# The first expert layer in six chunks of 384 tokens instead of nine of 256, with a chain of three steps

## The chip, the cores and the metric

The kernel runs on one core of one Trainium2 chip, as one program. The metric is the device time of one execution in microseconds (us): the median of the runs, and beside it the time of the one execution that was profiled. In the profile PE is TensorE (matmul), PEld its weight loads, DVE VectorE, ACT ScalarE, POOL GpSimd and SP SyncE.

## The reference

Three layers stand one behind the other. All inputs and results are float32.

```python
# attention: 4 batches, 8 heads, 576 tokens, head size 64, causal, with a decay bias
bias = -(cum[:, :, :, None] - cum[:, :, None, :])          # cum = cumsum(max(s, 0))
scores = where(causal, -1e9, scale * q @ k.T + minimum(bias, 0))
x = softmax(scores) @ v                                     # -> 2304 tokens x 512
# first expert layer: w_in 512 x 2048, w_out 2048 x 512, both in 64-bit floats in DRAM
h = x @ w_in
x = (h * cos(h)) @ w_out
# second layer: 8 experts, each w1 512 x 1024 and w2 1024 x 512, the best two for each token
noisy = x @ w_gate + log1p(exp(x @ w_noise)) * noise
top2, weights = best two of noisy, softmax over the two
out[token] += weight * (relu(x @ w1[e]) @ w2[e])            # for both experts e of a token
```

## The kernel before

Every float32 product is done as three passes on TensorE: each operand is split into a high part (a rounded copy that ScalarE writes) and a low part (the difference that VectorE or GpSimd writes), and high x high, high x low and low x high are summed in PSUM (`PASS`). So behind nearly each operand stand a copy on ScalarE and a subtraction on another engine.

**The order of the work** is the order in which Python issues it; each engine goes through its own list in that order. Three tables and loops set it.

- `front` (L179) runs attention: 16 pairs of heads with 5 units each, in a loop over t. Its copies to high parts are L287, the low parts L291, the copies of its results L440 and L443, its last product L437. In each turn it calls `moe.beside(t, N)` (L784), which hangs early work of the first expert layer beside it: loads and conversions of weight pieces, splits of x, and in the last turns the first six steps of the layer (one turn has two).
- `Moe1` (L710) is the first expert layer. Its unit of work, an item, is a chunk c of 256 tokens and a block f of 128 of the 2048 inner features. There are 144 items: the first three chunks are interleaved over the 16 blocks (48 items), since every new block needs weights that have just been converted; then come five chunks in order, and the last one runs backwards over f. `step()` (L918) issues one step: for item i the product L1 (L865, 12 matmuls of 256 columns), for item i-1 two copies out of PSUM on ScalarE (L879, L880) and `angle` on VectorE (L886: h minus a multiple of 2 pi), for item i-2 `cosine` on ScalarE (L890 Abs, L891 Sin with its table), for item i-3 `gate` (L895 on VectorE, L897 on ScalarE), for item i-4 `rest_of_gate` (L903 on VectorE), and for item i-LAG, LAG = 5, the product L2 (L905, two tiles of 128 tokens with three matmuls of 512 columns). Two PSUM banks hold L1's results.
- Weights of the first layer come as 64-bit floats; 32 pieces (w_in and w_out for each f) are converted in five steps in as many turns (`w_steps`, L749): Abs on ScalarE (L760), two operations on VectorE (L763, L764), two more (L767, L768), the high part on ScalarE (L773), the low part on VectorE (L778). `convert()` does the next step of each piece under way.
- When a chunk ends, `finish` (L946) copies it out, writes it to DRAM, transposes it tile by tile and makes the router's products, logits, best two, and places. `Router` works on groups of tiles (`GROUPS`), and GpSimd scatters the tokens of a group into the lists of the experts by indirect DMA (L695), two scatters for a tile.
- `Moe2` (L1039) is the second layer. A job is an expert and a number of tiles of 126 tokens from its list; each has 8 steps, one for each block of 128 inner features. A step has L1 (L1133), relu copies (L1136, L1137) and L2 (L1145); the weights of a later step are split on ScalarE (L1121) and on VectorE or GpSimd (L1122). So that the second layer can start before the first has ended, the first jobs work only on the tokens routed by then (`FIRST` tiles of 128): experts 0 and 1 with 3 tiles, then experts 2 to 7 with 5, then experts 0 and 1 again with the other 2. `meet` (L1260) joins the two layers: the last chunk's transposes, products and router work are hung on steps and tiles of the first job by a table (step, tile).

## Time and profile before

| | |
|---|---|
| median of 3 runs | 1158.11 us (1156.95 to 1158.71) |
| profiled execution | 1157.83 us, of which span 1156.1 us |
| TensorE busy | 1101.7 us (95%), 6988 instructions |
| VectorE busy | 722.2 us (62%) |
| ScalarE busy | 677.8 us (59%) |
| GpSimd busy | 474.2 us (41%) |
| moved by DMA | 148.98 MB, mean 129 GB/s |

The busy shares are means over the whole span, and the stages have different limits. Attention lasts to some 230 us, the first expert layer to some 680 us, the second to the end. Which engine sets the pace is read per stage: from the gaps on TensorE, and from what ended each.

### The profile page before, as it was taken

How to read it: one execution, taken by the hardware profiler on the slowest of the kernel's cores; microseconds unless marked ns; L12 is line 12 of the kernel's file. 1: busy time of each engine (PE TensorE's matmuls, PEld its weight loads, DVE VectorE, ACT ScalarE, POOL GpSimd, SP SyncE). 2: the span in 40 equal slices, each digit the busy share in tenths (PEclk: the TensorE clock that was granted, in tenths of full speed). 3: DMA queues.
4: the chain of work that ended last, by engine and by line, in shares of the span. 5: the costliest groups of instructions: out<-in, count | busy, mean ns of one | idle time of the engine just before them, and what ended most of it. 6: DMA issues, size and time to landing. Idle time of an engine off the chain costs nothing.

```text
span 1156.1 us, 20848 instructions
## 1 busy us (share of the span) xinstructions
PE 1101.7 (95%) x6988; PEld 972.3 (84%) x6988; DVE 722.2 (62%) x1811; ACT 677.8 (59%) x1744; POOL 474.2 (41%) x665
## 2 busy tenths in 40 slices
PE   5999889899999999999999999999999999999995
PEld 4887777787778999988898978999999989999884
DVE  5999999889988544465446676544444444445382
ACT  4999988877778666676667764423232323233241
POOL 4777877400002101006313158545454545445373
PEclk7999999999999999999999999999999999999998
DMA  6788977365552201102010347644444444434461
GB/s 170 204 224 243 260 222 217 131 175 146 156 150 44 92 1 56 42 14 57 1 56 20 101 123 211 196 142 134 133 135 133 134 135 134 138 113 135 130 209 39
DMA packets 167692, 148.98 MB, mean 129 GB/s; under 512 B 73912, under 2 KB 132696, under 8 KB 167576
## 3 DMA queue, kind: packets, MB, share of 16 engines
q1 hardware_dynamic: 154904, 119.17, 35.4%
q0 software_dynamic: 12672, 28.39, 7.9%
q8 instruction: 57, 0.93, 0.4%
q14 instruction: 59, 0.48, 0.2%
HBM read 120.50 MB, written 29.66 MB: 130 GB/s over the span
## 4 chain that ended last, share of the span: by engine, by line
PE 69%; DVE 11%; ACT 10%; issue 4%; DMA 3%; POOL 1%; SPq 1%; another core or an unknown queue 0%; POOLq 0%; DVEq 0%; ACTq 0%
PE bank L1133 18%; PE bank L1145 18%; PE bank L869 11%; PE bank L913 11%; PE bank L437 3%; PE bank L396 2%; DVE float32r L291 2%; DVE scratch L368 2%; PE bank L342 2%; ACT float32r L897 1%; PE bank L1093 1%; ACT float L891 1%; DVE float L767 1%; ACT float L760 1%; DVE float L768 1%
## 5 line engine op out<-in xcount | busy, mean ns | idle before, releaser
L1133 PE MATMUL bank<-float32r 128*128 128x252 f32 (+1 forms) x1536 | 240.5, 310 | 0.9 <-DVE float32r L1137 0.5
L1145 PE MATMUL bank<-float32r 128*126 128x512 f32 x960 | 235.5, 394 | 0.0
L1133 PEld LDWEIGHTS bank<-float32r 128*128 128x128 f32 x1536 | 230.3, 189 | 5.5 <-DVE float32r L1137 1.0
L1145 PEld LDWEIGHTS bank<-float32r 128*126 128x126 f32 x960 | 174.4, 187 | 36.5
L869 PE MATMUL bank<-float32r 128*128 128x256 f32 x1296 | 177.8, 286 | 5.4 <-ACT float L880 5.1
L869 PEld LDWEIGHTS bank<-float32r 128*128 128x128 f32 x1296 | 166.3, 190 | 17.8 <-ACT float L880 10.0
L913 PE MATMUL bank<-float32r 128*128 128x512 f32 x630 | 166.2, 394 | 2.4 <-DVE float32r L903 2.4
L1136 ACT ACTIVATE float32r<-bank 128x378 fp32r<-128x378 f32 (+1 forms) x128 | 55.7, 435 | 185.0 <-PE bank L1133 167.2
L824 POOL TENSOR_TENSOR float<-float 128x256 f32<-128x256 f32 x24 | 20.1, 845 | 274.9 <-DMA float<-xt 273.3
L1122 POOL TENSOR_TENSOR float32r<-late,float32r 128x512 fp32r<-128x512 f32 x60 | 77.8, 1297 | 128.4 <-ACT float32r L1121 127.9
L913 PEld LDWEIGHTS bank<-float32r 128*128 128x128 f32 x630 | 112.1, 189 | 21.8 <-DVE float32r L903 3.3
L1137 DVE SCALAR_TENSOR_TENSOR float32r<-bank,float32r 128x378 fp32r<-128x378 f32 (+1 forms) x128 | 61.8, 483 | 102.3 <-ACT float32r L1136 80.3
L886 DVE SCALAR_TENSOR_TENSOR float<-float 128x256 f32<-128x256 int32 x144 | 63.8, 443 | 54.7 <-ACT float L880 53.4
L287 ACT ACTIVATE float32r<-bank 128x512 fp32r<-128x512 f32 (+3 forms) x192 | 83.5, 478 | 15.7 <-PE bank L300 9.7
L1122 DVE TENSOR_TENSOR float32r<-late,float32r 128x512 fp32r<-128x512 f32 x60 | 77.7, 1294 | 24.1 <-ACT float32r L1121 24.0
L1102 DVE TENSOR_TENSOR float32r<-bank,float32r 128x504 fp32r<-128x504 f32 x40 | 27.3, 682 | 99.3 <-ACT float32r L1101 98.3
L1101 ACT ACTIVATE float32r<-bank 128x504 fp32r<-128x504 f32 x40 | 23.7, 593 | 109.8 <-PE bank L1093 103.8
L903 DVE TENSOR_TENSOR float32r<-float,float32r 128x256 fp32r<-128x256 f32 x144 | 62.5, 434 | 39.2 <-ACT float32r L897 35.5
L379 ACT ACTIVATE scratch<-scratch 128x256 f32<-128x256 f32 (+2 forms) x144 | 82.9, 583 | 6.2 <-POOL scratch L282 6.2
L388 POOL TENSOR_SCALAR scratch<-scratch 128x256 f32<-128x256 f32 (+2 forms) x144 | 82.7, 587 | 5.8 <-DVE scratch L386 2.1
L291 DVE TENSOR_TENSOR float32r<-bank,float32r 128x512 fp32r<-128x512 f32 (+4 forms) x160 | 81.8, 539 | 4.4 <-ACT float32r L287 3.2
L897 ACT ACTIVATE float32r<-float 128x256 fp32r<-128x256 f32 x144 | 58.5, 406 | 43.6 <-DVE float L895 41.6
(155 smaller groups left out, 1929.7 us busy)
## 6 DMA issues: line engine op xcount, KB each, us to landing
late<-in_moe_w_dram SPq DMA_DIRECT2D x120, 256.0 KB
float<-negcum SPq DMA_DIRECT2D x15, 768.0 KB
float<-in_moe_w_dram SPq DMA_DIRECT2D x40, 256.0 KB
xt<-scratch SPq DMA_DIRECT2D x32, 288.0 KB
float<-in_moe_w_in_dram SPq DMA_DIRECT2D x16, 512.0 KB
float<-in_moe_w_out_dram SPq DMA_DIRECT2D x16, 512.0 KB
float<-xt SPq DMA_DIRECT2D x48, 128.0 KB
float<-negcum SPq DMA_DIRECT2D x32, 144.0 KB
```

The lines of the kernel that those rows point to most:

```text
L287: nc.scalar.activation(hi, src, AF.Copy, scale=1.0 if sc is None else sc)
L291: nc.vector.tensor_tensor(lo, src, hi.bitcast(F32), ALU.subtract)
L379: nc.scalar.activation(sc, sc, AF.Exp, bias=m, scale=-1.0, accum_out=sm[:, hh, 0:1])
L388: nc.gpsimd.tensor_scalar(sc, sc, r[:, hh:hh + 1], 1.0, op0=ALU.mult, op1=ALU.mult)
L869: self.nc.tensor.matmul(ps, w[a][:, 128 * k:128 * k + 128], self.xs[c, k][b], start=(n == 0), stop=(n == 11))
L886: nc.vector.scalar_tensor_tensor(r, n, -TWO_PI, h, op0=ALU.mult, op1=ALU.add)
L897: nc.scalar.activation(h, r, AF.Copy)
L903: self.nc.vector.tensor_tensor(l, r, h.bitcast(F32), ALU.subtract)
L913: self.nc.tensor.matmul(self.acc[c][t], g[a][:, 128 * t:128 * t + 128], w[b], start=(first and n == 0), stop=(last and n == 2))
L1122: (nc.vector if kind else nc.gpsimd).tensor_tensor(l, r, h.bitcast(F32), ALU.subtract)
L1133: nc.tensor.matmul(ps, w[a][:, 128 * k:128 * k + 128], self.xT[q][b][:, k, c], start=(m == 0), stop=(m == 11))
L1145: self.nc.tensor.matmul(self.acc[q][t], h[a][:, ROWS * t:ROWS * t + ROWS], w[b], start=(f == 0 and n == 0), stop=(f == FB - 1 and n == 2))
```

## The change

The first layer's chunk gets 384 tokens (`CH`, three tiles, `TN`), so that there are six chunks and 96 items: two interleaved chunks (32 items), three in order, and the last one backwards. L1 has 12 matmuls of 384 columns, L2 nine of 512. The chain from L1 to L2 has three steps instead of five: `gate` and `high` of item i-2, `angle` and `cosine` of item i-1, `rest_of_gate` of item i-2 and L2 of item i-3 stand in one step, in a new order. The four conversion operations on VectorE go together, and one piece is begun per step. Attention's last five turns take one step each. The splits of x follow the new chunk size, and attention's buffers lie elsewhere to make room.

The router takes groups of 9, 3, 3 and 3 tiles. `finish` transposes by blocks of 128 features (three tiles in one bank); the router's products sum up over these blocks in one bank of their own, which logits, counts and totals use too (`list_bank`). The second layer's early jobs are experts 0 to 2 with two tiles each, and three later jobs take the rest of these experts with three tiles each: 11 jobs of 8 steps instead of 10. The last chunk's router work has three tiles, six scatters, in one place of the table.

```diff
-EARLY = 3 * ROWS
+EARLY = 2 * ROWS
 LIST = 2432
 SPARE = (LIST - CAP) // 128
-WORDS_R, WORDS, SHARED = 32800, 10400, 9200
-FIRST = 14
+WORDS_R, WORDS, SHARED = 33040, 9416, 10300
+CH, TN = 384, 3
+FIRST = 12
+SPLIT = 3
...
-    def products(self, bank, x):
-
-        ps = bank[:, 0:256]
...
+    def products(self, bank, k, x):
+
+        for a in range(2):
+            self.nc.tensor.matmul(bank[:, 0:CH], self.wg[:, k], x[a], start=(k + a == 0), stop=(k + a == 4))
+        if k == 3:
+            self.nc.scalar.activation(self.terms, bank[0:32, 0:CH], AF.Copy)
...
-                for e in range(2):
+                for e in range(SPLIT):
...
-    LAG = 5
+    LAG = 3
     PRE = 2
     ORDER = tuple(range(9))
-    GROUPS = {4: 10, 6: 4, 7: 2, 8: 2}
+    NC = 6
+    GROUPS = {2: 9, 3: 3, 4: 3, 5: 3}
...
-        self.items = [(c, f) for f in range(16) for c in range(3)] + [(c, f) for c in range(3, 8) for f in range(16)]
-        self.items += [(8, f) for f in range(15, -1, -1)]
-        self.at0 = {c: min(i for i, x in enumerate(self.items) if x[0] == c) for c in range(9)}
-        self.end = {c: max(i for i, x in enumerate(self.items) if x[0] == c) for c in range(9)}
+        last = self.NC - 1
+        self.items = [(c, f) for f in range(16) for c in range(2)]
+        self.items += [(c, f) for c in range(2, last) for f in range(16)] + [(last, f) for f in range(15, -1, -1)]
...
         def b():
             nc.vector.tensor_scalar(cf, cf, EXP_LO, EXP_HI, op0=ALU.max, op1=ALU.min)
             nc.vector.tensor_scalar(c, c, 3, 0x3FFFFFF8, op0=ALU.logical_shift_left, op1=ALU.bitwise_and)
-
-        def d():
             nc.vector.scalar_tensor_tensor(c, hi, TOP2, c, op0=ALU.bitwise_and, op1=ALU.bitwise_or)
             nc.vector.scalar_tensor_tensor(c, lo, 29, c, op0=ALU.logical_shift_right, op1=ALU.bitwise_or)
+            if last:
+                self.arena.free(self.rawtile[j])
...
-        return [a, b, d, e, g]
+        return [a, b, e, g]
...
-        for _ in range((1, 1, 1, 2, 1)[t - N + 2] if t >= N - 2 else 0):
+        if t >= N - 2:
             self.step()
...
+        run(self.gate, 2)
         run(self.copy, 1)
         run(self.L1, 0)
-        while len(self.conv) < 4 and self.nconv in self.raw and self.nconv < min(32, self.PRE + (2 * i + 2) // 3 + 2):
+        while len(self.conv) < 4 and self.nconv in self.raw and self.nconv < min(32, self.PRE + i + 3):
             self.conv.append(self.w_steps())
-        run(self.rest_of_gate, 4)
+        run(self.high, 2)
+        run(self.angle, 1)
+        run(self.cosine, 1)
+        run(self.rest_of_gate, 2)
         self.convert()
-        run(self.cosine, 2)
-        run(self.gate, 3)
-        run(self.angle, 1)
         run(self.L2, self.LAG)
...
+    def list_bank(self):
+        if not hasattr(self, "ps_p"):
+            self.ps_p = Banks(self.arena, 1)
+        return self.ps_p.tile()
...
+                steps = [ops[j:j + per] for j in range(0, len(ops), per)] + [place + adv]
+                steps += [scat[j:j + 2] for j in range(0, len(scat), 2)]
...
-    JOBS = [(e, 0, 3) for e in range(2)] + [(e, 0, 5) for e in range(2, E_)] + [(e, EARLY, 2) for e in range(2)]
+    JOBS = [(e, 0, 2) for e in range(SPLIT)] + [(e, 0, 5) for e in range(SPLIT, E_)]
+    JOBS += [(e, EARLY, 3) for e in range(SPLIT)]
...
+        if moe.i == N + 1:
+            moe.ps_h.close()
             E.step(0)
...
-    for at, fns in {(1, 0): (lambda: tr(0), lambda: tr(1), lambda: sp(0), lambda: sp(1), *moe.rest[0]), (1, 2): [lambda: E.blank(E.oldp)] * 6,
-                    (2, -1): (pr, moe.fin.close), (2, 1): (lg,), (2, 2): (head,), (3, -1): moe.rest[1], (3, 3): (ops("top"),),
-                    (4, 2): (ops("place"), ops("scat")), (5, 3): (ops("adv"), close)}.items():
+    for at, fns in {(1, 0): (each(tr, 0, 1), each(sp, 0, 1)), (1, 2): [lambda: E.blank(E.oldp)] * 6,
+                    (2, -1): (each(pr, 0, 1), each(tr, 2, 3), each(sp, 2, 3)), (3, -1): (each(pr, 2, 3), moe.fin.close),
+                    (3, 1): (lg,), (3, 2): (head,), (4, 2): (ops("top"),),
+                    (5, 2): (ops("place"), ops("adv"), ops("scat")), (5, 3): (close,)}.items():
```

**ScalarE at the end of attention.** In the rows before, L287 and L440 are attention's copies, L879 and L880 copies of item 0, L760 and L773 the weights' Abs and high parts.

```order
L287 ACTIVATE float32r<-bank_73 128x3x128
L879 ACTIVATE float_88<-bank_76 128x256
L880 ACTIVATE float_88<-bank_76 128x256
L760 ACTIVATE float_88<-float_88 128x512
L287 ACTIVATE float32r<-bank_74 128x8x64
L287 ACTIVATE float32r<-bank_75 128x2x64
L440 ACTIVATE scratch<-bank_80 128x2x256
L773 ACTIVATE float32r<-float_88 128x512 x2
```

After, the same attention copies are L289 and L442, those of item 0 L896 and L897; L907 and L908 are item 0's cosine, L767 and L780 the weights.

```order
L289 ACTIVATE float32r<-bank_73 128x3x128
L896 ACTIVATE float_88<-bank_76 128x384
L897 ACTIVATE float_88<-bank_76 128x384
L907 ACTIVATE float_88<-float_88 128x384
L908 ACT_TABLE_LOAD
L908 ACTIVATE float_88<-float_88 128x384
L780 ACTIVATE float32r<-float_88 128x512 x2
L767 ACTIVATE float_88<-float_88 128x512 x2
L289 ACTIVATE float32r<-bank_74 128x8x64
L289 ACTIVATE float32r<-bank_75 128x2x64
L442 ACTIVATE scratch<-bank_80 128x2x256
```

The cosine of item 0, with its table, and two high parts and two Abs of weights moved ahead of the three last copies shown.

**VectorE in the interleaved stretch.** Before, conversions (L763, L764, L767, L768, L778) and the gate's operations (L895, L886, L903) alternate, with two of a conversion's four operations in one step.

```order
L763 TENSOR_SCALAR float_88<-float_88 128x512
L764 TENSOR_SCALAR float_88<-float_88 128x512
L895 TENSOR_TENSOR float_88<-float_88 128x256
L886 SCALAR_TENSOR_TENSOR float_88<-float_88 128x256
L903 TENSOR_TENSOR float32r<-float_88,float32r 128x256
L767 SCALAR_TENSOR_TENSOR float_88<-float_88 128x512
L768 SCALAR_TENSOR_TENSOR float_88<-float_88 128x512
```

After, a step has gate (L912), angle (L903), rest of gate (L923), a low part (L785) and all four operations of the next piece.

```order
L912 TENSOR_TENSOR float_88<-float_88 128x384
L903 SCALAR_TENSOR_TENSOR float_88<-float_88 128x384
L923 TENSOR_TENSOR float32r<-float_88,float32r 128x384
L785 TENSOR_TENSOR float32r<-float_88,float32r 128x512
L770 TENSOR_SCALAR float_88<-float_88 128x512
L771 TENSOR_SCALAR float_88<-float_88 128x512
L772 SCALAR_TENSOR_TENSOR float_88<-float_88 128x512
L773 SCALAR_TENSOR_TENSOR float_88<-float_88 128x512
```

The gate's operations have 384 columns, and the dependent ones of a piece stand directly behind each other.

**GpSimd at the last chunk's scatters, in the second layer's first jobs.** Before, four scatters (L695, each behind a small memset) stand between two splits of weights (L1122); four others, of the chunk before, stand earlier.

```order
L1084 DMA float_88<-out_dram,float_88 126x512
L692 MEMSET float_88 1x1
L695 DMA lists<-float_88 19456x3
L692 MEMSET float_88 1x1
L695 DMA lists<-float_88 19456x3
L692 MEMSET float_88 1x1
L695 DMA lists<-float_88 19456x3
L692 MEMSET float_88 1x1
L695 DMA lists<-float_88 19456x3
L1122 TENSOR_TENSOR float32r<-late,float32r 128x512
```

After, there are six in a row (L697), of which the last four stand here, ahead of a split (L1147).

```order
L694 MEMSET float_88 1x1
L697 DMA lists<-float_88 19456x3
L694 MEMSET float_88 1x1
L697 DMA lists<-float_88 19456x3
L694 MEMSET float_88 1x1
L697 DMA lists<-float_88 19456x3
L694 MEMSET float_88 1x1
L697 DMA lists<-float_88 19456x3
L1147 TENSOR_TENSOR float32r<-float_88,float32r 128x512
L1047 IOTA cnt 1x8
```

The split behind the scatters is that of the first weight of the second job, and the iota of the overflow's count follows it.

## Rows read from the trace of the kernel before

**Rows 1.** Page, section 4: share of the chain that ended last, by line
```profile
PE bank L1133 18%; PE bank L1145 18%; PE bank L869 11%; PE bank L913 11%; PE bank L437 3%; PE bank L396 2%; DVE float32r L291 2%; DVE scratch L368 2%; PE bank L342 2%; ACT float32r L897 1%; PE bank L1093 1%; ACT float L891 1%; DVE float L767 1%; ACT float L760 1%; DVE float L768 1%
```

**Rows 2.** Timeline of PE, where the layers meet: start, us, instruction [idle before, releaser]
```profile
662.51 1.59 PE L869 MATMUL bank<-float32r 128*128 128x256 f32 x12
...
670.01 1.20 PE L913 MATMUL bank<-float32r 128*128 128x512 f32 x4 [2.09 <-DVE float32r L903]
...
678.75 1.55 PE L1133 MATMUL bank<-float32r 128*128 128x378 f32 x8
...
1115.18 1.67 PE L1133 MATMUL bank<-float32r 128*128 128x252 f32 x12 [0.52 <-DVE float32r L1137]
```

**Rows 3.** Timeline of PE in the chunks that run in order
```profile
560.03 1.59 PE L869 MATMUL bank<-float32r,more 128*128 128x256 f32 x12
561.46 1.55 PE L913 MATMUL bank<-float32r 128*128 128x512 f32 x6
562.85 1.59 PE L869 MATMUL bank<-float32r,more 128*128 128x256 f32 x12
```

**Rows 4.** Timeline of PE in the interleaved stretch, and the first item behind it
```profile
261.48 1.69 PE L869 MATMUL bank<-float32r 128*128 128x256 f32 x12 [0.57 <-ACT float L880]
...
271.01 1.69 PE L869 MATMUL bank<-float32r 128*128 128x256 f32 x12 [0.58 <-ACT float L880]
...
369.69 1.59 PE L869 MATMUL bank<-float32r 128*128 128x256 f32 x12
```

**Rows 5.** Window: A:B, us, busy (x) of PE PEld DVE ACT POOL, clock, DMA, GB/s
```profile
300.00:320.00 20.00, 18.85 (x118) 16.12 (x117) 18.08 (x41) 15.48 (x41) 0.00 (x0) 1.00 0.53 158
```

**Rows 6.** Timeline of DVE: angle of item 0, then one stretch of the interleaved chunks
```profile
225.40 0.42 DVE L886 SCALAR_TENSOR_TENSOR float<-float 128x256 f32<-128x256 int32 x1
...
334.26 0.68 DVE L767 SCALAR_TENSOR_TENSOR float<-float 128x512 int32<-128x512 int32 x1
334.98 0.69 DVE L768 SCALAR_TENSOR_TENSOR float<-float 128x512 int32<-128x512 int32 x1
335.59 0.42 DVE L763 TENSOR_SCALAR float<-float 128x512 f32<-128x512 f32 x1
336.04 0.43 DVE L764 TENSOR_SCALAR float<-float 128x512 int32<-128x512 int32 x1
336.38 0.42 DVE L895 TENSOR_TENSOR float<-float 128x256 f32<-128x256 f32 x1
336.72 0.42 DVE L886 SCALAR_TENSOR_TENSOR float<-float 128x256 f32<-128x256 int32 x1
337.29 0.42 DVE L903 TENSOR_TENSOR float32r<-float,float32r 128x256 fp32r<-128x256 f32 x1 [0.15 <-ACT float32r L897]
337.63 0.69 DVE L767 SCALAR_TENSOR_TENSOR float<-float 128x512 int32<-128x512 int32 x1
```

**Rows 7.** Timeline of ACT: the load of the sine's table
```profile
227.64 1.28 ACT L891 ACT_TABLE_LOAD   x1
```

**Rows 8.** Timeline of PE at attention's last products: first and last of three gaps
```profile
224.40 0.91 PE L437 MATMUL bank<-float32r 128*128 128x320 f32 x5 [0.82 <-ACT scratch L440]
...
229.82 1.57 PE L437 MATMUL bank<-float32r 128*128 128x320 f32 x10 [0.99 <-ACT scratch L443]
```

**Rows 9.** Timeline of DVE in the first job of the second layer
```profile
683.44 2.11 DVE L1056 MEMSET float<- 128x512 f32 x4
...
695.25 0.53 DVE L632 CAST float<-float 128x4 f32<-128x4 uint32 x1
```

**Rows 10.** Timeline of POOL: the first of four scatters, and the split behind them
```profile
698.29 1.03 POOL L695 DMA_INDIRECT lists<-float  x1 [1.18 <-DVE float L632]
...
703.15 1.31 POOL L1122 TENSOR_TENSOR float32r<-late,float32r 128x512 fp32r<-128x512 f32 x1
```

**Rows 11.** Windows near the program's start, same columns as Rows 5
```profile
12.00:16.00 4.00, 1.51 (x12) 1.16 (x12) 1.06 (x5) 0.00 (x0) 0.78 (x2) 0.76 1.09 245
...
20.00:24.00 4.00, 2.67 (x15) 1.87 (x13) 2.96 (x12) 2.70 (x11) 3.57 (x6) 0.50 0.93 252
```

More of the change, by code (lines that the diff above doesn't have):

```diff
@@ L754, in w_steps @@
         lo, hi = self.raw[j][:, :, 0], self.raw[j][:, :, 1]
-        h, l = self.w[j % 2, j // 2] = [self.arena.tile([128, 512], F32R) for _ in range(2)]
+        last = j >= 28
+        home = self.more if j >= 22 else None
+        h, l = self.w[j % 2, j // 2] = [self.arena.tile([128, 512], F32R, home) for _ in range(2)]
         cf = self.raws.tile([128, 512], name="c", bufs=4)
@@ L778, in g @@
             nc.vector.tensor_tensor(l, cf, h.bitcast(F32), ALU.subtract)
-        return [a, b, d, e, g]
+            if last:
+                self.arena.free(cf)
+        return [a, b, e, g]
     def convert(self):
@@ L786, in convert @@
         self.conv = [x for x in self.conv if x]
-        if self.nconv == 32 and not self.conv and self.raws:
-            self.raws.close()
-            self.raws = None
+        if self.nconv == 32 and not self.conv:
             self.more.open = False
@@ L816, in x_split @@
         nc = self.nc
-        r = self.xr.tile([128, 2, 256], F32, name="xr")
-        for h in range(2):
-            nc.sync.dma_start(out=r[64 * h:64 * h + 64],
-                              in_=self.xt[k, h, :, 256 * c:256 * c + 256].rearrange("(a p) t -> p a t", a=2))
-        a, b = r[:, 0], r[:, 1]
+        own = not self.xr
+        if own:
+            a, b = (self.arena.tile([128, CH]) for _ in range(2))
+        else:
+            r = self.xr.tile([128, 2, CH], F32, name="xr")
+            a, b = r[:, 0], r[:, 1]
+        for h in range(2):
+            src = self.xt[k, h, :, CH * c:CH * c + CH].rearrange("(a p) t -> p a t", a=2)
+            if own:
+                for i, x in enumerate((a, b)):
+                    nc.sync.dma_start(out=x[64 * h:64 * h + 64], in_=src[:, i])
+            else:
+                nc.sync.dma_start(out=r[64 * h:64 * h + 64], in_=src)
         def add():
@@ L826, in high @@
         def high():
-            self.xs[c, k] = [self.arena.tile([128, 256], F32R) for _ in range(2)]
+            self.xs[c, k] = [self.arena.tile([128, CH], F32R) for _ in range(2)]
             nc.scalar.activation(self.xs[c, k][0], a, AF.Copy)
@@ L832, in low @@
             nc.vector.tensor_tensor(l, a, h.bitcast(F32), ALU.subtract)
+            if own:
+                self.arena.free(a, b)
         return add, high, low
@@ L840, in open @@
         nc.gpsimd.memset(self.halfpi, TWO_PI / 4)
-        for c in range(9):
+        for c in range(self.NC):
             self.finish(c)
-            if c >= 3:
+            if c >= 2:
                 for k in range(4):
@@ L895, in gate, with high @@
         nc.vector.tensor_tensor(r, r, self.hp.pop((c, f)), ALU.mult)
-        h, l = self.gt[c, f] = [self.gtp.tile([128, 256], F32R, name=f"g{z}") for z in "hl"]
+    def high(self, c, f):
+        nc, r = self.nc, self.r[c, f]
+        h, l = self.gt[c, f] = [self.gtp.tile([128, CH], F32R, name=f"g{z}") for z in "hl"]
         nc.scalar.activation(h, r, AF.Copy)
@@ L908, in L2 @@
         if first:
-            self.acc[c] = [self.arena.bank() for t in range(2)]
+            self.acc[c] = [self.arena.bank() for t in range(TN)]
         g, w = self.gt.pop((c, f)), self.w[1, f]
-        for t in range(2):
+        for t in range(TN):
             for n, (a, b) in enumerate(PASS):
@@ L1294, in meet @@
     ev()
-    for r in (moe.ps_h, moe.el, moe.gtp):
+    for r in (moe.el, moe.gtp):
         r.close()
```

134 lines of the change are left out of this document (65 added, 69 removed).

## The prediction

> **What bounds the kernel now.** I read the chain of waits first, then the windows, and last the timelines of each engine at the joints between the stages. The two matmul lines of the second layer alone, L1133 and L1145, are 36% of the chain [rows 1]; 36% of 1156.1 us is 416 of the 465 us that this layer takes from 678.75 [rows 2]. So there TensorE is the bound. So it is from the third chunk of the first layer to its end: twelve matmuls of L1 and then six of L2 follow each other without a gap [rows 3]. In the interleaved stretch it is not. Three steps take 271.01 − 261.48 = 9.53 us [rows 4], while TensorE needs 3 × 2.82 = 8.46, and VectorE is busy for 18.08 of 20 us [rows 5]. So the change is to be priced in three stretches with different limits. All is summed against the profiled execution: span 1156.1, time 1157.83, which is 0.28 under the median of the runs, 1158.11.
>
> **Price of a step.** Before, L1 with 256 columns takes 561.46 − 560.03 = 1.43 (119 ns a matmul) and six of L2 with 512 columns take 562.85 − 561.46 = 1.39 (232 ns), together 2.82 [rows 3]. No matmul of 384 columns stands in this stretch; it lies between these two, and the mean is 175.5 ns: 12 × 0.1755 = 2.11. L2 has nine instead of six: 9 × 0.232 = 2.09. The step is 4.20. 96 × 4.20 = 403 against 144 × 2.82 = 406: the wider chunk by itself is worth 3 us. A matmul of 384 columns costs 119 to 232 ns by these rows whatever it follows; since a column costs 0.465 ns at 256 and 0.453 at 512, 174 to 179 is likely, ±0.03 a step and ±2.5 us over 96 steps.
>
> **Stretch 1: end of attention and interleaved chunks, to the first L1 that is not interleaved (369.69 before [rows 4]).** VectorE's work: operations on 256 columns are issued every 0.34 us (336.38, 336.72), two-input ones on 512 every 0.61 to 0.72 [rows 6]; 384 columns lie between, 0.47. In the new step: gate 0.47, angle 0.47, rest of gate 0.47, low part of a weight piece 0.61, and the four conversion operations together 0.45 + 0.45 + 0.72 + 0.61 = 2.23. The wait for ScalarE's high part was 0.15 [rows 6]; it now stands directly behind the gate, and I take 0.20. Sum 4.45, against TensorE's 4.20. VectorE still bounds, but 768 columns cost 2 × 4.45 = 8.90 instead of 9.53. Over some 13 such sets this gains 8 us.
>
> Against that stands the start. ScalarE now does both cosine operations of item 0, behind them the load of the sine table, and two high parts and two Abs of weights, ahead of attention's last copies. Before, those copies come first. The cosine needs angle(0), and that stands on VectorE behind two pieces' eight conversion operations, as it did before: it started at 225.40 [rows 6], with 384 columns it ends near 226.2. From there ScalarE needs 0.5 + 1.28 (table load [rows 7]) + 0.53 + 1.1 + 1.2 (estimates from the widths, by operations of 0.51 to 0.64) before the copies of attention's last head pairs: the first is read near 232.3, where TensorE went on with attention at 224.40 [rows 8]. The same order comes back one step later: the high part of item 0 waits for a gate behind two more pieces' eight operations, and the second attention product starts near 242.1 instead of 229.82 [rows 8]. TensorE stands idle there for about 7.6 + 6.3 = 13.9 us, where before it had three gaps of about a us, 0.82 and 0.99 the outer two [rows 8], some 3 in all: 10.9 us more. VectorE, too, has little to do in the gaps and loses about 9.
>
> So the third step begins near 243.5. From there 26 to 27 steps of VectorE's 4.45 lead to the low part of the last L1 weight, 359.2 to 363.7; I take 363, because the gap falls into the middle of a step. Two steps of TensorE more (8.4) give 371. If TensorE bounded, 29 × 4.20 would give 365.4; if the waits for ScalarE double, 374. **+1.3 us.**
>
> **Stretch 2: to the second layer's second L1 (678.75 [rows 2]).** Before 309.1. Of 662.51 − 369.69 = 292.8 [rows 2, 4], 95 steps × 2.82 are 267.9, and 24.9 is work of other kinds on TensorE (transposes, router). After: 63 × 4.20 = 264.6. Of the 24.9, one tile fewer is routed here (−1.15) and a 0.83 stall goes, so 22.9. Count and total of the router now share one bank, and each waits until the other is read: three times 0.4 (a wait that no row shows; bounds 0 and 3 × 0.9). The drain is one L1, four L2 of 2.09 and an L1 of 252 columns, 2.11 + 8.36 + 1.41 + 0.1 = 12.0; the stalls in the old one (2.09 at 670.01 [rows 2] the largest) go with the shorter chain of lag 3. Sum 300.7: **−8.4 us**, ±2.
>
> **Stretch 3: the second layer (464.5 us before, from 678.75 to the last matmul).** The tiles are the same 40, so TensorE has no more columns. The smaller L1 ahead of the anchor, more transposes and a last router chunk of three tiles put 2.1 more behind the anchor; the stall of 0.52 at 1115.18 [rows 2] goes: +1.6. But the first three jobs give TensorE only two tiles a step, 2.8 us instead of 4.2, while the other engines' work in these steps stays or grows:
> - Six memsets of 0.53 (four take 2.11 [rows 9]) stand on VectorE ahead of what the router's products need. The step was long enough to hide them; in the short one 2.4 us look out.
> - The place operations wait for the top operations: 0.9.
> - GpSimd has six scatters instead of four in one stretch. Four took 703.15 − 698.29 = 4.86 [rows 10], so six take 7.3. Behind them waits the split of a weight of step 8 (1.31 [rows 10]), ahead of them VectorE's placing (695.25 to 698.29, 3.04 [rows 9]). 3.04 + 7.3 + 1.31 = 11.65 against 6.4 of TensorE's work in between: 5.3.
> - The count for the overflow stands behind the scatters' iota and holds a bank: 0.9. Five gathers in the second job: 0.6.
>
> Together 10.1, of which none need show (if the splits are early enough) and 16 could (if nothing overlaps). **+11.7 us.** Loading the third expert's weights twice costs nothing on TensorE as long as the DMA keeps ahead; its transfers lie beside TensorE's work, and if that cover were gone, the upper end has room for it.
>
> Sum: 1157.83 + 1.3 − 8.4 + 11.7 = **1162.4**. The stretch after the last matmul is unchanged.
>
> **Rivals.**
> *A, faster: the gap at the end of attention doesn't open.* If ScalarE's wait for angle(0) ends before attention's next unit is due, as it would if L1(0) were issued earlier against attention than the order suggests, the 10.9 us stay away: 1162.4 − 10.9 = 1151.5. For it: the gap rests on a chain of four waits worked out, not seen. Against: engines issue in order, and the copies stand behind the cosine. It decides from 4 us of gap on: with less than 4 of the 10.9, the time falls under 1156.
> *B, no change: one hole of the early jobs doesn't show,* above all the scatters' 5.3, if the split behind them is needed a step later than I count: 1157.1.
> [...]
>
> [...]
>
> **How the numbers follow.** Forecast 0.40, own range 1160.5 to 1166; A 0.27; B 0.21; C 0.12. No change means within 0.2%, 2.3 us, about what a measurement of this kernel can tell. Slower is the forecast and C: 0.52; same is B: 0.21; faster is A: 0.27. The range goes from A's 1151 to 1172, C with the upper ends of stretches 1 and 2, and leaves less than 2 in 10.
>
> **What would show it.** Right: two gaps of TensorE before attention's last products (5 us or more each), ended by ScalarE's copies; the first L1 that isn't interleaved near 371; the second layer's second L1 near 672; a gap of some 5 us in the second layer's first 60 us, released by a GpSimd split. Wrong: no such gaps at the end of attention (A), or steps of the interleaved stretch at 4.20 and not 4.45, bounded by TensorE; steps of the later chunks far from 4.20 would overturn the largest term at once.

## The result, and the profile after

The changed kernel takes 1172.06 us (median, 1170.92 to 1174.84) against 1157.84 beside it: ratio 1.0126, 95% interval 1.0107 to 1.0146, 14.2 us slower. The direction was forecast, the size was three times the forecast 4.6, and the time lies 0.06 us above the end of the range, 1172. The profiled execution took 1170.92 us, span 1169.2, 13.1 more than before. By the prediction's own marks:

| stretch | before | after | difference | forecast |
|---|---|---|---|---|
| to item 0's L1 | 219.53 | 222.65 | +3.1 | 0 |
| from there to the first L1 in order | 150.16 | 153.78 | +3.6 | +1.3 |
| to the second layer's second L1 | 309.06 | 301.54 | −7.5 | −8.4 |
| to the end of the last matmul | 464.57 | 479.15 | +14.6 | +11.7 |
| behind it | 12.8 | 12.1 | −0.7 | 0 |

Traced again, the same kernel gave every mark down to the last matmul within 0.1 us; other traces of the same attention lie further apart, as told under the experiments. The timeline of TensorE of the changed kernel at the end of attention (start, us, instruction, in brackets the idle time before and what ended it) answers to [rows 8]:

```profile
222.65 2.25 PE L886 MATMUL bank<-float32r 128*128 128x384 f32 x12
...
235.18 2.77 PE L439 MATMUL bank<-float32r 128*128 128x320 f32 x10 [7.15 <-ACT scratch L442]
237.75 3.62 PE L886 MATMUL bank<-float32r 128*128 128x384 f32 x12
245.20 2.77 PE L439 MATMUL bank<-float32r 128*128 128x320 f32 x10 [3.83 <-ACT scratch L445]
```

The two gaps stand where they were forecast, ended by ScalarE's copies of attention. The second product comes 22.55 us behind item 0's first L1, and the prediction had 22.6 (242.1 − 219.53). The second gap is 2.5 us shorter than the forecast 6.3, because the matmuls ahead of it took that much longer. Behind each gap the same matmuls take longer: ten of 320 columns 2.77 us against 1.57 at [rows 8]. The windows (busy us of each engine, then the granted clock) say why:

```profile
234.00:238.00 4.00, 2.82 (x11) 2.82 (x12) 3.43 (x7) 1.89 (x5) 0.00 (x0) 0.50 0.00 0
...
700.00:704.00 4.00, 3.77 (x25) 3.58 (x25) 2.62 (x9) 2.50 (x6) 2.36 (x5) 0.68 0.03 5
```

The granted clock was 0.50 in the window behind the 7.2 us gap, and 0.68 in the mean from 700 to 704 us, behind two gaps in the second layer. TensorE's steps after that, and the end of the interleaved stretch, answer to [rows 3, 4]:

```profile
253.39 2.27 PE L886 MATMUL bank<-float32r 128*128 128x384 f32 x12
255.49 2.24 PE L933 MATMUL bank<-float32r 128*128 128x512 f32 x9
257.57 2.27 PE L886 MATMUL bank<-float32r 128*128 128x384 f32 x12
...
329.65 2.01 PE L886 MATMUL bank<-float32r,more 128*128 128x384 f32 x10 [0.31 <-DVE more L785]
...
357.11 2.04 PE L886 MATMUL bank<-float32r,more 128*128 128x384 f32 x10 [0.90 <-DVE more L785]
...
368.26 2.01 PE L886 MATMUL bank<-float32r,more 128*128 128x384 f32 x10 [2.48 <-DVE more L785]
...
376.43 2.27 PE L886 MATMUL bank<-float32r 128*128 128x384 f32 x12
```

L1 is 2.10 (forecast 2.11), L2 2.08 (2.09): the price of 384 columns by the mean of its two neighbours was right. From 253.39 to 324.65 TensorE goes through 17 steps of 4.19 us without a wait. Its first wait for a low part of a weight on VectorE is the one at 329.65, and the gaps at the end are waits for the same. VectorE's own timeline there, and GpSimd's beside it:

```profile
349.67 0.55 DVE L912 TENSOR_TENSOR float<-float 128x384 f32<-128x384 f32 x1
...
354.14 0.55 DVE L912 TENSOR_TENSOR float<-float 128x384 f32<-128x384 f32 x1
354.61 1.37 DVE L903 SCALAR_TENSOR_TENSOR float<-float 128x384 f32<-128x384 int32 x1
...
359.23 1.37 DVE L912 TENSOR_TENSOR float<-float 128x384 f32<-128x384 f32 x1
```

```profile
354.27 1.30 POOL L839 TENSOR_TENSOR float<-float 128x384 f32<-128x384 f32 x1 [130.95 <-DVE float L773]
358.99 1.19 POOL L839 TENSOR_TENSOR float<-float 128x384 f32<-128x384 f32 x1 [3.42 <-DMA float<-xt]
```

VectorE's step is 354.14 − 349.67 = 4.47 us. Four times in the last steps GpSimd adds the halves of the next chunk's x, and each time the operation of VectorE beside it takes 0.8 us longer (1.37 for 0.55): 3.2 us on VectorE, which the prediction did not count. The kernel before has four such adds at this place too, where they cost VectorE four times 0.54, 2.2 us:

```profile
348.49 0.42 DVE L895 TENSOR_TENSOR float<-float 128x256 f32<-128x256 f32 x1
348.82 0.96 DVE L886 SCALAR_TENSOR_TENSOR float<-float 128x256 f32<-128x256 int32 x1
```

Last, TensorE at the start of the second layer, answering to [rows 2]:

```profile
674.28 3.85 PE L933 MATMUL bank<-float32r 128*128 128x512 f32 x9 [2.07 <-ACT float32r L917]
677.97 1.57 PE L1158 MATMUL bank<-float32r 128*128 128x252 f32 x12
...
688.18 0.91 PE L596 MATMUL bank<-float32r 128*128 128x384 f32 x3 [1.59 <-DVE float32r L997]
...
698.47 0.17 PE L641 MATMUL bank<-float 128*128 128x24 bf16 x1 [1.02 <-DVE float L634]
...
700.23 0.29 PE L652 MATMUL bank<-float 128*128 128x8 bf16 x6 [1.47 <-DVE float L686]
...
709.99 1.44 PE L1158 MATMUL bank<-float32r 128*128 128x252 f32 x10 [1.61 <-POOL cnt L1047]
...
714.66 2.54 PE L1158 MATMUL bank<-float32r 128*128 128x252 f32 x12 [1.83 <-DVE float32r L1162]
```

From 677.97 on these and three smaller gaps (0.28, 0.25, 0.65) are 8.7 us; four groups of matmuls at the lower clock (2.54 instead of 1.57 here) cost 3.4 more.

### The profile page after: what moved, and what is told of

The parts are those of the page before. It is cut to its first block, busy times and chain, and to the rows that moved or that the text cites. A ratio compares the mean times of both kernels' runs of the same rounds, so it can differ in the third digit from the quotient of the medians.

```text
span 1169.2 us, 19352 instructions
## 1 busy us (share of the span) xinstructions
PE 1102.7 (94%) x6388; PEld 979.7 (84%) x6388; DVE 725.5 (62%) x1667; ACT 663.5 (57%) x1515; POOL 488.9 (42%) x661
## 4 chain that ended last, share of the span: by engine, by line
PE 68%; DVE 16%; issue 5%; DMA 4%; ACT 4%; POOL 3%; SPq 0%; POOLq 0%; DVEq 0%; ACTq 0%
PE bank L1170 17%; PE bank L1158 17%; PE bank L933 12%; PE bank L886 12%; PE bank L439 3%; DVE float L772 2%; DVE scratch L370 2%; DMA float<-negcum 2%; DVE float32r L293 2%; PE bank L398 2%; DVE float L912 1%; PE bank L344 1%; ACT float32r L917 1%; PE bank L1118 1%; DVE float L771 1%
## 5 line engine op out<-in xcount | busy, mean ns | idle before, releaser
L1158 PE MATMUL bank<-float32r 128*128 128x252 f32 (+1 forms) x1536 | 243.5, 311 | 4.3 <-DVE float32r L1162 1.8
L1158 PEld LDWEIGHTS bank<-float32r 128*128 128x128 f32 x1536 | 231.7, 190 | 9.5 <-POOL float32r L1147 2.7
L886 PE MATMUL bank<-float32r 128*128 128x384 f32 x792 | 153.5, 342 | 0.0
L933 PE MATMUL bank<-float32r 128*128 128x512 f32 x594 | 149.4, 396 | 2.1 <-ACT float32r L917 2.1
L886 PEld LDWEIGHTS bank<-float32r 128*128 128x128 f32 x792 | 141.7, 192 | 4.0
L1147 POOL TENSOR_TENSOR float32r<-late,float32r 128x512 fp32r<-128x512 f32 x66 | 85.8, 1301 | 127.9 <-ACT float32r L1146 127.3
L1147 DVE TENSOR_TENSOR float32r<-late,float32r 128x512 fp32r<-128x512 f32 x88 | 111.8, 1270 | 33.6 <-ACT float32r L1146 32.4
L933 PEld LDWEIGHTS bank<-float32r 128*128 128x128 f32 x594 | 111.6, 190 | 23.0 <-ACT float32r L917 2.5
L839 POOL TENSOR_TENSOR float<-float 128x384 f32<-128x384 f32 x16 | 17.2, 1076 | 245.2 <-DVE float L773 130.9
L289 ACT ACTIVATE float32r<-bank 128x512 fp32r<-128x512 f32 (+3 forms) x192 | 82.3, 481 | 20.0 <-PE bank L302 13.3
L1146 ACT ACTIVATE float32r<-late 128x512 fp32r<-128x512 f32 x154 | 89.2, 623 | 1.7 <-DMA late<-in_moe_w_dram 1.7
L439 PE MATMUL bank<-float32r 128*128 128x320 f32 (+2 forms) x448 | 77.8, 316 | 11.0 <-ACT scratch L442 7.1
L903 DVE SCALAR_TENSOR_TENSOR float<-float 128x384 f32<-128x384 int32 x96 | 55.4, 577 | 42.9 <-ACT float L897 42.7
```

The costliest lines, as they stand in the source:

```text
L289: nc.scalar.activation(hi, src, AF.Copy, scale=1.0 if sc is None else sc)
L439: nc.tensor.matmul(ps[:, c:n], v4[i][:, j, hh], t[a][:, j, hh, c:n], start=(m == 0), stop=(m == 2 * len(terms) - 1))
L886: self.nc.tensor.matmul(ps, w[a][:, 128 * k:128 * k + 128], self.xs[c, k][b], start=(n == 0), stop=(n == 11))
L933: self.nc.tensor.matmul(self.acc[c][t], g[a][:, 128 * t:128 * t + 128], w[b], start=(first and n == 0), stop=(last and n == 2))
L1146: nc.scalar.activation(h, r, AF.Copy)
L1147: (nc.vector if kind else nc.gpsimd).tensor_tensor(l, r, h.bitcast(F32), ALU.subtract)
```

## Experiments

All ratios are against the kernel before, run beside them on the same chip; the changed kernel stands at 1.0126, and at 1.0125 (1.0110 to 1.0141) when it was run again.

**The conversions beside attention, in two steps again.** In the changed kernel:

```diff
-STAGES = (34, 39, 44, 49), (49, 54, 59, 64)
+STAGES = (29, 34, 39, 44, 49), (44, 49, 54, 59, 64)
...
-        return [a, b, e, g]
+        return [a, b, e, g] if j >= 2 else [a, b, d, e, g]
```

> The changed kernel, with the conversion of the two early weight pieces beside attention in two VectorE steps again (two operations in one unit of attention, two in the next); everything else as changed. Theory: in the changed kernel all four operations of a piece stand in one unit of attention, take 3.3 to 3.9 us there beside GpSimd's work, and TensorE waits 3.3 us at 122.8 and 2.7 us at 165.7 and runs at the lower clock behind each; so item 0's first L1 goes from 222.65 back to about 219.5 and the time falls by 3 us, to about 1169. Rival: attention is late because of its other loads (q and k read into another part of memory, three ring buffers of 384 columns instead of four of 256): then the two gaps stay, and the time stays within 1 us of 1172.

Measured 1168.83 us, ratio 1.0118 (1.0102 to 1.0133): not told apart from the changed kernel, though a gain of 3 us is not excluded either. TensorE's gap did shrink from 3.31 at 122.76 to

```profile
123.02 0.55 PE L302 MATMUL bank<-ident,scratch 128*128 128x128 f32 x3 [1.03 <-DVE float32r L293]
```

but three others of 1.0 stand in attention, and item 0's L1 came at 222.29. The converse, in the kernel before (the two halves of a conversion joined for the two early pieces, in four stages that begin five turns later):

> The kernel before, with the four conversion operations of the two early weight pieces together in one unit of attention; nothing else changed. Theory: this part of the change alone makes attention 3 us longer; item 0's first L1 goes from 219.5 to about 222.5, and the time from 1157.8 to about 1161. Rival: attention was late for another part of the change; the time stays within 1 us of 1157.8.

Measured 1158.51 against 1155.59, ratio 1.0023 (1.0014 to 1.0032): 2.9 us, as the theory had it. The gap of the changed kernel is there too:

```profile
122.64 0.90 PE L300 MATMUL bank<-ident,float 128*128 128x128 f32 x3 [3.04 <-DVE float32r L291]
```

So the joined operations cost 3 us where all else is as before. The four gaps of 1.0 us that stay in the changed kernel when they are parted are no loss against the kernel before, which has four of them too, one at the same place:

```profile
121.80 0.55 PE L300 MATMUL bank<-ident,float 128*128 128x128 f32 x3 [1.02 <-DVE float32r L291]
```

What differs in the traces is the clock behind these gaps. Windows inside attention (columns as above) of the kernel before, the changed kernel and the run with the conversions parted, and of that last one a shorter window behind its gap at 123.02:

```profile
60.00:215.00 155.00, 141.96 (x1111) 119.78 (x1112) 144.90 (x525) 139.71 (x409) 120.46 (x205) 1.00 0.77 221
60.00:215.00 155.00, 141.43 (x1084) 120.23 (x1081) 141.66 (x511) 135.51 (x398) 116.15 (x192) 0.97 0.85 219
60.00:215.00 155.00, 142.02 (x1086) 119.87 (x1086) 142.03 (x512) 136.62 (x399) 116.91 (x194) 0.98 0.84 220
...
124.00:127.00 3.00, 3.00 (x16) 2.60 (x16) 2.53 (x9) 1.24 (x5) 1.52 (x4) 0.50 1.05 222
```

With the rest at 1.00, a mean of 0.97 over these 155 us stands for about 10 us at 0.50, one of 0.98 for about 7. TensorE is busy throughout in the shorter window, so that by estimate 7 us at 0.50 lose some 3 against 1.00, about what item 0's L1 is late (222.29 against 219.53). Why the clock was at 0.50 behind a gap of 1.03 us here, and at 1.00 behind that of 1.02 in the kernel before, is open. Splits at other turns were tried:

```diff
-SPLITS = (27, 32, 35, 40, 45, 47, 52, 55)
+SPLITS = (27, 30, 32, 35, 37, 40, 42, 47)
```

> The kernel with the early conversions in two steps again, with the eight splits of x beside attention at turns 27, 30, 32, 35, 37, 40, 42, 47, as the first ones were before, and not from 27 to 55. Attention stayed 2.5 us long in the trace with the conversions alone undone. Theory: the rest of attention's 2.8 us more comes from where the splits of 384 columns fall beside the early conversions; then item 0's first L1 comes 2 us earlier, some 201.5 to 202 us behind the matmul at 18 us, and the time falls by 2 us against the conversions alone. Rival: it comes from the splits' longer operations themselves (1.02 against 0.73 us on GpSimd, 0.55 against 0.42 on VectorE, one each), wherever they stand: no change.

Measured 1167.98, ratio 1.0099 (1.0085 to 1.0114). The ratio is lower, but its interval meets that of the run before; four gaps of 1.03 stay, the mean clock from 60 to 215 us is 0.98 again, and item 0's L1 came at 223.42, no earlier.

**The gap at the end of attention.**

```diff
-        self.convert()
         if t == N - 3:
...
             self.step()
+        self.convert()
```

> The changed kernel, with the conversions of a turn issued behind the turn's step of the first layer instead of ahead of it, in attention's last turns; everything else as changed. Theory: the gap at the end of attention comes from angle(0) and gate(0) standing behind eight conversion operations on VectorE. Angle(0) then starts about 2.9 us earlier, gate(0) directly when ScalarE's copies are done: the first gap of 7.2 us becomes 4 to 5, the second of 3.8 closes, and the lower clock behind it goes. As VectorE and TensorE bound the interleaved stretch nearly equally, 4 to 7 of that remain: 1165 to 1168. Rival: the interleaved stretch ends with VectorE's conversions whatever its start (VectorE only trades one idle time for another): the first chunk in order starts within 1 us of 376.4, and the time stays at 1172.

Measured 1169.59, ratio 1.0123 (1.0108 to 1.0139): no change, as the rival had it. TensorE's gaps:

```profile
227.15 0.33 PE L398 MATMUL bank<-ident,scratch 128*128 128x128 f32 x1 [2.93 <-DVE float32r L293]
...
233.90 0.91 PE L439 MATMUL bank<-float32r 128*128 128x320 f32 x5 [2.51 <-ACT scratch L442]
...
237.57 1.54 PE L439 MATMUL bank<-float32r 128*128 128x320 f32 x5 [2.76 <-DVE float32r L293]
```

The first L2 came 24.3 us behind item 0's L1 instead of 28.7, but the first L1 in order 152.8 instead of 153.8: of 4.4 us 1.0 is left. That VectorE takes the rest was tested by leaving out its low parts of weights as well:

> The kernel with the conversions issued behind the step in attention's last turns, and without the low parts of the first layer's weight pieces from the third on: VectorE's subtraction L785 is left out, and the matmuls read the high part twice. Theory: VectorE's work bounds the interleaved stretch, which is why the earlier start (4.4 us at the first L2) gave 1.0 at its end. Without 0.61 of 4.45 us a step TensorE's 4.18 bounds; the gaps of 0.9 and 2.5 us at its end go, and the first chunk in order starts about 7 us earlier after item 0's first L1 than in the changed kernel (153.8 us behind it there, about 147 here). Rival: the stretch's end is fixed by the loads of weights or by the chain of waits between gate, high part and rest: then it stays within 2 us of 153.

Measured 1162.05, ratio 1.0056 (1.0042 to 1.0069); the first L1 in order came 144.2 us behind item 0's, 8.6 earlier than with the conversions moved alone, and TensorE's steps were 4.19 us to the end of the stretch. That VectorE's work sets when this stretch ends is shown. Moving the same work to the idle GpSimd instead (`nc.gpsimd` for `nc.vector` in `g`):

> The changed kernel, with the low part of each weight piece of the first layer (all but the two early ones) on GpSimd, which is idle in the interleaved stretch, instead of on VectorE. Theory: VectorE is the bound of this stretch; 0.61 of its 4.45 us a step go, TensorE's 4.18 a step bound it then, the gaps of 0.9 and 2.5 us at its end go, and the first chunk in order starts 4 us earlier: the time falls by 3 to 5 us. Rival: GpSimd's 1.3 us a piece slow VectorE's operations that run beside them (0.77 and 1.37 instead of 0.69 were seen beside GpSimd's in attention): what VectorE gains it loses, and the time stays within 1 us or rises.

Measured 1176.9, ratio 1.0176 (1.0162 to 1.0190): 6 us slower than the changed kernel. VectorE and GpSimd of that run:

```profile
302.73 1.68 DVE L773 SCALAR_TENSOR_TENSOR float<-float 128x512 int32<-128x512 int32 x1
```

```profile
302.30 1.56 POOL L785 TENSOR_TENSOR float32r<-float,float32r 128x512 fp32r<-128x512 f32 x1 [3.29 <-ACT float32r L780]
```

VectorE's operation took 1.68 us, against 0.69 with GpSimd idle, and ended 0.55 us behind GpSimd's. The step went from 4.47 to 4.85 us: 0.61 less for the work moved, 0.99 more for this longer operation. Both edits together:

> The edit of the low parts on GpSimd together with that of the conversions issued behind the step in attention's last turns. Theory: the earlier start by the second edit was worth 4.4 us at the first L2 and only 1.0 at the end of the interleaved stretch, since VectorE bounded it. With VectorE relieved TensorE bounds, and the 4 us stay: the time is 3 to 4 us under that of the low parts alone, some 7 under the changed kernel. Rival: something other than VectorE's work fixes the end of the stretch (the loads of the weights); then it ends at the same time as with one edit.

1179.63, ratio 1.0190 (1.0176 to 1.0204): worse again, a miss of the theory for the same reason.

**The clock at the front.**

```diff
         moe.beside(t, N)
+        if t in (N - 1, N):
+            if t == N - 1:
+                fill = arena.bank()
+            w = moe.w[0, 0][0]
+            for _ in range(26 if t == N - 1 else 14):
+                nc.tensor.matmul(fill, w[:, 0:128], w, start=True, stop=True)
...
```

> The changed kernel with 26 and 14 matmuls of 512 columns more, whose result nobody reads, in the two gaps at the end of attention (6.0 and 3.2 us of work in gaps of 7.2 and 3.8). Theory: the granted clock stays at its upper level through the gaps; the products behind them take 1.56 and 2.25 instead of 2.77 and 3.6 us, and the first L2 comes 4 to 5 us earlier. As VectorE bounds the interleaved stretch, 1 us of that is left at its end, and the time falls by 0 to 2 us: the lower clock there is not what cost the time. Rival: the lower clock at the front is paid in full, and the time falls by 4 us or more.

Measured 1171.5, ratio 1.0131 (1.0112 to 1.0150). Behind the first gap the granted clock held, 1.00 from 226 to 242 us; behind the second it did not, 0.57 in the mean from 242 to 250:

```profile
226.42 6.09 PE L512 MATMUL bank<-float32r 128*128 128x512 f32 x26
233.74 1.57 PE L439 MATMUL bank<-float32r 128*128 128x320 f32 x10 [1.22 <-ACT scratch L442]
...
243.78 2.77 PE L439 MATMUL bank<-float32r 128*128 128x320 f32 x10 [3.14 <-ACT scratch L445]
```

The second product still came 22.6 us behind item 0's L1, with a wait for ScalarE's copy ahead of it, and the first L2 28.9 against 28.7, not 4 to 5 earlier as the theory had it. The first L1 in order came 153.8 us behind item 0's, as without the edit. So the lower clock behind the first gap costs nothing: the copy comes no sooner. The lower clock behind the second gap was not taken away by this run; that most of an earlier start is lost again by the end of the stretch is what the run with the conversions moved shows. The reference beside it:

> The changed kernel once more, unaltered, beside the two other runs on one chip: the reference for them, and a second trace of the same instructions. Theory: item 0's first L1 comes at 222.5 to 225 us (five traces with the same attention gave 222.6 to 225.3), so that attention's 3 us against the one trace of before are partly the spread of attention from run to run; the rest of the span behind it agrees with the first trace within 1 us. Rival: it comes at 222.65 within 0.3 again, and attention is 3 us longer every time.

1171.75 us, ratio 1.0125; item 0's L1 at 222.63, the rival's outcome. Still, the eight traces with this attention reach from 221.2 to 225.3, and the two with that of the kernel before have 218.1 and 219.5. The ranges don't meet, so attention is longer, but a single trace gives the amount to some 3 us only, and the table's first row with it.

**The second layer.** The count for the overflow moved from step 6 of the second layer to step 20:

> The changed kernel, with the count for the overflow taken 14 steps later in the second layer, away from the scatters; everything else as changed. Theory: VectorE's queue waited 6.1 us for GpSimd's iota, which stands behind six scatters and a weight split; that gives the TensorE gaps of 1.6 and 1.8 us at 710 and 714.7, and the lower clock behind them, some 1.7. The time falls by 4 to 5 us, to about 1167.5. Rival, as the prediction had it: the gap comes from the weight split that stands behind the scatters, with the count only 0.9 of it: then most of the gap stays and the time falls by 1 us at most.

Measured 1179.23, ratio 1.0197 (1.0180 to 1.0214): slower, against both. The gap of 1.61 grew to 3.18, now ended by GpSimd's weight split, so the split behind the scatters binds as well as the count; and at its new place the count waits for its iota again:

```profile
709.81 2.50 PE L1158 MATMUL bank<-float32r 128*128 128x252 f32 x10 [3.18 <-POOL float32r L1147]
...
759.52 0.65 PE L1118 MATMUL bank<-ident,float 126*128 126x126 f32 x4 [4.06 <-DVE float32r L1127]
```

Then the scatters two by two in three steps, the iotas early:

> The changed kernel, with the six scatters of the last router chunk in three pairs, one in each of three steps of the second layer, and the two iotas of the overflow's count issued on GpSimd in the first job's second step, so that VectorE's count waits for no scatter. Theory: with the scatters out of the way of the weight splits the gap of 3.2 us that stayed when the count alone was moved goes, and with the iotas early the 1.8 us of the count go as well, and the lower clock behind them, 1 to 2 us: the time falls by 4 to 6 us, to about 1165 where the changed kernel takes 1170 to 1172. Rival: the gaps belong to the short early steps as such (two tiles give TensorE 2.8 us a step, the weights' splits need as much on each engine); then other waits of the same size come up in the same 20 us, and the time falls by 1 us at most.

Measured 1174.0, ratio 1.0143 (1.0124 to 1.0163): the rival's outcome. Other waits came up in the same 20 us:

```profile
713.61 1.43 PE L1163 MATMUL bank<-float32r 128*128 128x252 f32 x10 [1.32 <-POOL float L694]
717.59 1.45 PE L1163 MATMUL bank<-float32r 128*128 128x252 f32 x10 [0.93 <-POOL float32r L1152]
723.91 0.65 PE L1123 MATMUL bank<-ident,float 126*128 126x126 f32 x4 [3.48 <-DMA float<-xnat,float]
```

The memsets moved into the first layer's last two steps:

> The changed kernel, with the six memsets of the second layer's row buffers on VectorE in the last two steps of the first layer instead of the second layer's second step. Theory: the gap of 1.6 us at 688 goes (the router's products wait for VectorE behind these memsets), and no new one comes, since VectorE had 2.4 us of idle time in each of these steps: 1.5 us less. Rival: they delay the gate's last low parts there, and the gap of 2.1 us at 674 grows by as much: no change.

Measured 1169.1, ratio 1.0104 (1.0086 to 1.0122); the gap of 1.59 is gone, one of 0.38 came, and the stretch is 477.2 instead of 479.2. It fits the theory, but the ratio's interval meets the changed kernel's.

Now the job table itself. In the changed kernel, back to three tiles and two experts (`EARLY = 3 * ROWS`, `SPLIT = 2`, the list of jobs and the last chunk's table to match):

> The changed kernel with the second layer's jobs as before: experts 0 and 1 early with three tiles, then experts 2 to 7 with five, then the rest of the first two with two; the last chunk's router work a step earlier in the table, as before, and on the two banks of the transposes from its logits on. Six chunks of 384, the chain of three steps and the front stay as changed. Theory: the gaps behind the second layer's start (8.7 us, and 3.4 of lower clock) come from the short steps of the two-tile jobs; with 4.2 us a step the router's work, memsets, scatters and count lie beside TensorE's work again, and the stretch from the second layer's second L1 to the last matmul falls from 478 to 466 to 468 us: 10 to 12 us less, about 1160. Rival: the gaps come from the last chunk's three tiles (six scatters, longer transposes), whatever the early jobs: then most of them stay, and the time falls by 3 us at most.

Measured 1167.12, ratio 1.0090 (1.0073 to 1.0107); the stretch is 472.0 us, 7.1 less: most of what the theory had (10 to 12), and more than the rival's 3. Two larger gaps stay or are new:

```profile
720.35 2.18 PE L1158 MATMUL bank<-float32r 128*128 128x378 f32 x11 [2.67 <-DVE float32r L1127]
...
1126.24 1.66 PE L1158 MATMUL bank<-float32r 128*128 128x252 f32 x12 [2.18 <-DVE float32r L1162]
```

And in the kernel before, the change's job table alone:

```diff
-    JOBS = [(e, 0, 3) for e in range(2)] + [(e, 0, 5) for e in range(2, E_)] + [(e, EARLY, 2) for e in range(2)]
+    JOBS = [(e, 0, 2) for e in range(SPLIT)] + [(e, 0, 5) for e in range(SPLIT, E_)]
+    JOBS += [(e, EARLY, 3) for e in range(SPLIT)]
...
```

> The kernel before with the changed kernel's job table alone: experts 0 to 2 early with two tiles, then the five others, then the rest of the three with three tiles; nine chunks of 256 and the chain of five steps stay. Theory: the short early steps alone open the gaps behind the second layer's start, and the stretch from the second layer's second L1 to the last matmul goes from 464.6 to 472 to 476 us: the time goes to 1165 to 1168. Rival: they need the last chunk's three tiles with their six scatters in a row to show; with two tiles there the stretch stays within 3 us of 464.6.

Measured 1165.88 against 1157.65, ratio 1.0074 (1.0060 to 1.0088): 8.2 us, and the stretch is 474.5 us, 9.9 more, as the theory had it. The largest gaps:

```profile
688.64 1.44 PE L1135 MATMUL bank<-float32r 128*128 128x252 f32 x10 [0.82 <-POOL float32r L1124]
...
694.85 0.17 PE L640 MATMUL bank<-float 128*128 128x16 bf16 x1 [3.38 <-DVE float L633]
...
703.53 1.44 PE L1135 MATMUL bank<-float32r 128*128 128x252 f32 x10 [1.56 <-POOL float32r L1124]
```

The short early jobs, with the tables that go with them, cost 7 to 10 us of this stretch, with chunks of 256 too: shown from both sides. Last, three undoings together (three tiles, conversions in two steps, conversions behind the step):

> Three edits together: early jobs of three tiles, the early conversions in two steps, the conversions behind the step in attention's last turns. Theory: 10 to 12 us from the second layer and 1 to 2 from the front: 1157 to 1160, which leaves what the interleaved stretch and attention still lose against what the later chunks gain; not faster than the kernel before. Rival: the parts overlap (an earlier end of the first layer meets the same late lists), and the sum is under 8 us.

Measured 1163.35, ratio 1.0063 (1.0049 to 1.0077): half of the loss is back, as the rival had it (under 8 us), and no version beat the kernel before. Against the run with the three-tile jobs alone (1.0090) the two other edits give some 3 us. In the trace item 0's L1 stands at 219.55, as in the kernel before, and the clock inside attention is nearly back:

```profile
60.00:215.00 155.00, 142.26 (x1102) 120.33 (x1101) 143.36 (x519) 137.54 (x404) 119.18 (x199) 0.99 0.84 220
```

## Why the prediction was right in direction and wrong in size

- **The step that failed first is one that the prediction didn't have.** Its sum begins at the end of attention. That the four conversion operations of the early pieces go together also beside attention was costed at nothing without naming what hides it. VectorE is busy for 144.90 of 155 us in attention before; there the four take 3.3 to 3.9 us in one unit, and TensorE waits for 3.3 and 2.7 us, with the clock at 0.50 behind both. That part alone costs the kernel before 2.9 us. In the changed kernel attention is 3.1 us longer in the trace. With the conversions parted its gaps are those of the kernel before, and what is left of the loss, nothing in one trace, 2.8 and 3.9 us in two, goes with the lower clock.
- **Stretch 1: right mechanism, term mis-sized by 2.3 us.** The two gaps, their releasers and their places came as forecast (11.0 us of idle time against 13.9), and two of VectorE's steps take 8.95 us against 8.90. One of the prediction's signs of being wrong came true for 17 steps: TensorE's steps there were 4.19 us, bounded by TensorE, which caught up with VectorE by 0.28 us a step; from 329.65 on it waits for VectorE, and VectorE sets the end. What was missed is GpSimd's four adds at the end, beside which four of VectorE's operations take 3.2 us longer. The last wait for a low part ended 145.6 us behind item 0's L1, and the prediction had 143.5; the adds are more than that difference, but no run moved them. The gap itself costs little: with an earlier start 1.0 of 4.4 us was left.
- **Stretch 2 was right**: −7.5 against −8.4. The drain's 2.07 us stall, which was to go with the shorter chain, stayed; it is now the wait for the gate's high part, and 1.6 us of lower clock stand behind it.
- **Stretch 3: the mechanism is right, the term mis-sized by 2.9 us.** Gaps of 8.7 us were measured against 10.1 forecast (memsets 1.6 against 2.4, placing 2.5 against 0.9, scatters and count 3.4 against 6.2, gathers 0.9 against 0.6). The sum has no term for the lower clock behind these gaps, 3.4 us; that was left to rival C. TensorE is the bound there, so it is paid. The other 2.5 us, against 1.6 forecast, were not traced further.
- **Rivals.** A did not happen: the gap opened. Had it not, the time would hardly have been 10.9 less, as the run with the earlier start shows. B did not. C, the lower granted clock of [rows 11] (0.50 from 20 to 24 us) again behind later gaps, had 0.12 of the chances and set the upper end of the range, 1172; no run shows the amount that the range takes for it. What the runs showed is the lower clock in the second layer, where it cost 3.4 us, inside attention, where the prediction had no gap, behind the stall at 674, where nine matmuls of L2 took 3.85 us against 2.24, and at the end of attention, where it cost nothing behind the first gap and was not tested behind the second.

In the changed kernel's trace the granted clock was 0.50 behind the gaps of 7.2, 3.8, 3.3, 2.7 and 2.1 us and behind two pairs of gaps of 1.0 to 1.8 us, and 1.00 behind the single one of 1.6 at 688. What it cost depended on the bound of the stretch.

## What to carry to other kernels

A chain made shorter by joining steps makes longer blocks in the queue of each engine it passes, and these must be priced wherever the same code runs, beside the stage before as well: here four conversion operations together took 3.3 to 3.9 us of VectorE in attention, and TensorE waited 3.3 and 2.7 us. Before filling an early stage with shorter jobs, add up what the other engines must do in one job step: here a step of 2.8 instead of 4.2 us left router work, scatters and weight splits in the open, and moving the count or the scatters only moved the wait. Where TensorE is the bound, look in the trace for a lower clock behind a gap and count the two together: in the second layer here 8.7 us of gaps brought 3.4 us more. On an engine that is the bound, look also at what runs beside it: here four adds on GpSimd came with 3.2 us more on VectorE.

## What the runs showed of the hardware

In these traces operations of VectorE took longer beside an operation of GpSimd with two inputs: 1.37 instead of 0.55 us beside an add of 1.30, 1.68 instead of 0.69 beside a subtraction of 1.56, and in the kernel before 0.96 instead of 0.42 beside an add of 1.00. So the move of 0.61 us of VectorE's work to an idle GpSimd made each step 0.38 us longer.
